# A decode kernel of four layers on one core: GELU as one activation, norms from two sums, first queries by pairs, and w4 with consecutive rows per partition

## The chip, the core and the metric

The kernel runs on one core of one Trainium2 chip. The metric is the time of one execution on the device in microseconds (us); shorter is better. The engines that matter here are PE (TensorE, matmuls; its weight loads stand apart as PEld), DVE (VectorE), ACT (ScalarE), and SP (SyncE), which here only issues transfers (DMAs) from the chip's main memory (HBM) into the on-chip memory (SBUF). Matmuls write PSUM, the accumulator memory.

## The reference

One token of 640 numbers passes through four layers: attention over a cache, a mixer, the same attention again, the same mixer again.

```python
x = x + A(layernorm(x)); x = x + B(layernorm(x))
x = x + A(layernorm(x)); x = x + B(layernorm(x))

# A: W = 4096 last cache rows, 32 heads of 192
q = x @ wq
p = softmax(einsum(q, k_cache[W]) * 192 ** -0.5)
return einsum(p, v_cache[W]) @ wo

# B: with one position the shifted parts of the first half are zero,
# so x1 = x, and what is left is
return x + gelu(layernorm(x) @ w3, approximate=True) @ w4     # w3 640x1536, w4 1536x640
```

Weights, caches and x are bf16. K and V of one head's window are 1.5 MB each.

## The kernel before, in words

**Slots and transfers.** The on-chip memory holds 15 slots of 1.5 MB (`slot`, each 128 partitions by 6144 bf16), one tile `half` of half that size, and two tiles for wo. All large transfers are issued by SP, in one order, which `plan` writes down: for each group of four heads the next group's K between this group's V, wo of the group after its second V, and w3 and w4 (`load_w34`, L131 to L144) last. A load (L111 for K and V) is issued when its slot has come free; SP waits there, and everything behind it on SP waits too. The queue behind SP works through the loads one after the other. Between uses `half` holds the softmax's scratch, the queries Q8 and the output O_sb; at the end of an attention it takes the last rows of w4.

**Attention.** It walks over eight groups of four heads. `qproj` makes a group's queries: 30 matmuls (L288) of 128x128 pieces of wq with one column, a mask (Xq, L292), a spreading matmul (Qrep, L296) and Q8 (L299). DVE turns K over in two halves per head (L311), `kmm` makes the scores (L351, 12 matmuls per head, each on a quarter of PE's columns; even and odd heads use different quarters). `soft_a` to `soft_c` make the softmax of the four heads, `pv_rows` multiplies with V (L458), `evac_rows` scales and turns the result, and `outproj` multiplies with wo (L521), summing over all groups in y_ps. The last group of an attention does its last two heads by `pv_cols` (L432, L443), whose result `evac_cols` scales (L471 to L475). The second attention walks the groups backwards and starts with the last group of the first, whose K (already turned over) and V have stayed in their slots; for these four heads the scores need no transfer, only the queries, and each head that is done frees a slot for a next K.

**Norms.** `ln_tot` takes three sums over the 640 numbers: the mean on DVE (L236), the squares on ACT (L239) and the negative mean on ACT (L241, Identity); a matmul with ones (L243) adds them over the partitions. The variance is completed by tensor_scalar on DVE (L256, L264, L268), and its inverse root by Ln and Exp on ACT (L248, L250). The mixer has two norms in a row, with two such pairs.

**Mixer.** 60 matmuls with w3 (L627) give the 1536 hidden values as 12 columns hT_ps; seven instructions on ACT and DVE make their GELU from Square and Exp (L632 to L640); 60 matmuls with w4 (L644) follow, 36 from a slot and the last 24 from `half`. w3 piece (kc, fc) is 128 consecutive columns; w4 row fc*128 + p lies in partition p, 12 separate rows per partition. The first w3 slot comes free when hT_ps is done, the second after y2T.

ACT's table set is loaded once (L159).

Of the kernel before, what the change touches and what calls it, by code (L numbers as in the profile page):

```python
# [16 lines left out]
P = 128  # L17
G = 4
ACT_TABLE_SET = 6
GELU_C = 0.044715  # L20
GELU_A = -2.0 * (2.0 / 3.141592653589793) ** 0.5
NSLOTS = 15
# [3 lines left out]
def kernel(  # L26
# [14 lines left out]
    nc = tc.nc  # L41
    _, _, D = A_x.shape
# [22 lines left out]
    eps = 1e-5  # L65
# [14 lines left out]


    x_bf = const.tile([ND, P], BF16, name="x_bf")
    nc.scalar.dma_start(x_bf[:], A_x.rearrange("a b (n p) -> (a b n) p", p=P))
# [74 lines left out]

    nc.scalar.add_instruction(mybir.InstLoadActFuncSet(  # L159
        name=nc.get_next_instruction_name(), act_func_set_id=ACT_TABLE_SET, ins=[], outs=[]))  # L160
    ident = const.tile([P, P], F32, name="ident")
# [70 lines left out]

    def ln_tot(src, neg):
        stats = sm.tile([P, 3], F32, tag="ln_stats", name="stats")
# [7 lines left out]
        tot_ps = psm.tile([P, 3], F32, tag="psm", name="tot_ps")  # L242
        nc.tensor.matmul(tot_ps[:], lhsT=ones[:], rhs=stats[:], start=True, stop=True)  # L243
        return tot_ps

    def inv_sqrt(tot_ps, bias, a, name):
        lnv = sm.tile([P, 1], F32, tag=name + "_ln", name="lnv")
        nc.scalar.activation(lnv[:], tot_ps[:, 1:2], ACTF.Ln, bias=bias[:], scale=a)  # L248
# [4 lines left out]
    def ln_stats(src):  # L253
        tot_ps = ln_tot(src, 1.0)
        nt = sm.tile([P, 1], F32, tag="ln_nt", name="nt")
        nc.vector.tensor_scalar(  # L256
            out=nt[:], in0=tot_ps[:, 0:1], scalar1=tot_ps[:, 2:3], scalar2=eps,
            op0=ALU.mult, op1=ALU.add)
        return tot_ps, inv_sqrt(tot_ps, nt, 1.0, "ln_rstd")

    def ln_ln_stats(src):
        tot_ps = ln_tot(src, 1.0 + eps)
        n2 = sm.tile([P, 1], F32, tag="ln_n2", name="n2")
        nc.vector.tensor_scalar(  # L264
            out=n2[:], in0=tot_ps[:, 0:1], scalar1=tot_ps[:, 2:3], scalar2=eps * eps,
            op0=ALU.mult, op1=ALU.add)
        nt = sm.tile([P, 1], F32, tag="ln_nt", name="nt")
        nc.vector.tensor_scalar(  # L268
            out=nt[:], in0=n2[:], scalar1=1.0 / (1.0 + eps), scalar2=eps - eps * eps / (1.0 + eps),
            op0=ALU.mult, op1=ALU.add)  # L270
        r2 = inv_sqrt(tot_ps, n2, 1.0 + eps, "ln_r2")
        return tot_ps, inv_sqrt(tot_ps, nt, 1.0, "ln_rstd"), r2

# [6 lines left out]
    Q_t = {}  # L280
    nq = [0]

    def qproj(g, xn_bf):
# [182 lines left out]

    def evac_cols(g, pr):
        osb, rl = sm.tile([P, 2, 3], BF16, name="osb"), sx[g]["rl"]
        osb_t[g] = osb
        O_ps = Oc_t[g][:, 0:8].rearrange("p (a b) -> p a b", a=2)  # L470
        nc.vector.tensor_tensor(  # L471
            out=osb[:, pr, 0:3:2], in0=O_ps[:, pr, 0:4:3], in1=rl[:, 2 * pr:2 * pr + 2], op=ALU.mult)
        nc.vector.tensor_tensor(
            out=osb[0:TB, pr, 1:2], in0=O_ps[0:TB, pr, 1:2], in1=rl[0:TB, 2 * pr:2 * pr + 1], op=ALU.mult)
        nc.vector.tensor_tensor(  # L475
            out=osb[TB:P, pr, 1:2], in0=O_ps[TB:P, pr, 2:3], in1=rl[TB:P, 2 * pr + 1:2 * pr + 2], op=ALU.mult)

# [38 lines left out]

    def outproj(g, pr, y_ps, first, last):
        osb = osb_t[g]
        for t in range(3):
            for n in range(ND):  # L520
                nc.tensor.matmul(  # L521
                    y_ps[:, n:n + 1], lhsT=wo_t[g][:, 3 * pr + t, n * P:(n + 1) * P],
                    rhs=osb[:, pr, t:t + 1],
                    start=(first and t == 0 and n == 0), stop=(last and t == 2),
                    skip_group_check=True)


    def attention(order, xT_cur, xT_new, keep, loads):
# [23 lines left out]
        tot_ps, rstd = ln_stats(xT_cur)  # L552
        xn_bf = sm.tile([P, ND], BF16, name="xn_bf")
# [19 lines left out]
        for n, g in enumerate(order[:-1]):  # L573
# [19 lines left out]
            if ahead_h is not None:  # L593
                outproj(g, 0, y_ps, n == 0, False)
                outproj(g, 1, y_ps, False, False)
# [4 lines left out]
        outproj(g, 0, y_ps, False, False)  # L600
        outproj(g, 1, y_ps, False, False)
        ahead("wo", gz)
# [13 lines left out]
    def mixer(xT_cur, xT_new):  # L616
# [13 lines left out]
        free.append(mlp["ab"][0])  # L630
        gu = sm.tile([P, NF], F32, name="gu")
        nc.scalar.activation(gu[:], hT_ps[:], ACTF.Square)  # L632
# [7 lines left out]
        nc.vector.tensor_tensor(out=hT[:], in0=ge[:], in1=hT_ps[:], op=ALU.mult)  # L640
        y2T_ps = psm.tile([P, ND], F32, tag="psm", name="y2T_ps")
# [28 lines left out]
    x2 = const.tile([P, ND], F32, name="x2")  # L670
    mixer(x1, x2)
    for g in first[:-2]:
# [6 lines left out]
    x4 = const.tile([P, ND], F32, name="x4")  # L679
    mixer(x3, x4)  # L680

# [35 lines left out]
```

## Time and profile before

| what | value |
|---|---|
| median of 3 runs | 534.06 us (533.92 to 534.87) |
| profiled execution | 534.18 us, span in the profile 532.3 us |
| busy share of the span | PE 59%, PEld 28%, DVE 53%, ACT 7% |
| DMA | 218.76 MB, mean 411 GB/s |
| mean granted TensorE clock | 0.672 |
| K and V loads | 60 each, 1.5 MB, 28.1 us from issue to landing (median) |

The span is cut into 40 slices of 13.3 us; a row of digits gives the busy tenths in each. The chain of waits follows the work that ended last back from the end, at each step to what released it. In a group or a timeline, a line reads: start, duration, engine, line of the program, operation, what it writes and reads, shapes, count, and in brackets how long the engine had been idle and who released it. "Issue to landing" is the time from SP's issue of a transfer to the moment its last byte is there. Durations of matmuls are modelled and overlap; the starts tell the rate.

### The profile page before, as it was taken

The page shows a single profiled execution, that of the slowest core. Times are in us where ns is not written, and L with a number is a line of the kernel's source. Part 1 is how long each engine was busy: PE and PEld are TensorE (multiplying, and loading weights), DVE is VectorE, ACT ScalarE, POOL GpSimd, SP SyncE. Part 2 cuts the span into 40 slices and gives each one's busy share as a digit, 9 for nine tenths or more (in the row PEclk, how much of TensorE's full clock was granted, in tenths as well). Part 3 has the DMA queues.
Part 4 walks back from the last instruction along what each step waited for, and adds up shares of the span by engine and source line. Part 5 has one row for each costly group of instructions (what it writes and reads, how often), then busy time and mean ns, then how long its engine had stood idle before and what let it go on. Part 6 is the DMA issues. An engine that isn't in the chain of part 4 may idle for free.

```text
span 532.3 us, 8132 instructions
## 1 busy us (share of the span) xinstructions
PE 316.7 (59%) x3597; PEld 151.1 (28%) x3597; DVE 280.6 (53%) x413; ACT 36.3 (7%) x113; POOL 2.1 (0%) x11
## 2 busy tenths in 40 slices
PE   1154756584656747555576677766565657454674
PEld 0011223141322313222155323333321314122254
DVE  4176565465645557264422476775736447365322
ACT  1001010010100001010011101010101001010011
POOL 1000000000000000000000000000000000000000
PEclk9998766656576665757665776768665765657655
DMA  8999999999999999999999899999999999999995
GB/s 348 428 426 423 420 428 424 428 423 425 422 425 426 422 424 426 424 425 422 422 407 338 326 415 428 421 424 425 423 425 422 426 428 423 423 425 425 420 406 193
DMA packets 26151, 218.76 MB, mean 411 GB/s; under 512 B 2692, under 2 KB 7300, under 8 KB 10116
## 3 DMA queue, kind: packets, MB, share of 16 engines
q1 hardware_dynamic: 26106, 218.25, 98.4%
q8 instruction: 28, 0.46, 0.3%
q14 instruction: 7, 0.06, 0.0%
q10 hardware_dynamic: 10, 0.00, 0.0%
HBM read 218.24 MB, written 0.00 MB: 410 GB/s over the span
## 4 chain that ended last, share of the span: by engine, by line
DMA 71%; PE 14%; DVE 12%; issue 1%; ACT 1%; SPq 0%; DVEq 0%
DMA slot<-in_A_v_cache_dram 37%; DMA slot<-in_A_k_cache_dram 34%; DVE slot L311 8%; PE S_ps L351 7%; PE y_ps L521 1%; PE qT_ps L288 1%; PE O_ps L458 1%; PE O_ps L432 1%; PE O_ps L443 1%; PE hT_ps L627 1%; PE y2T_ps L644 1%; DVE pm L367 1%; DVE half L389 0%; SPq L104 0%; PE OX_ps L496 0%
## 5 line engine op out<-in xcount | busy, mean ns | idle before, releaser
L311 DVE STREAM_TRANSPOSE slot<-slot 128x1536 uint32<-128x1536 uint32 x120 | 206.8, 1755 | 80.1 <-DMA slot<-in_A_k_cache_dram 80.1
L351 PE MATMUL S_ps<-slot,half 128*8 128x512 bf16 x768 | 172.6, 565 | 113.7 <-DVE slot L311 112.0
L351 PEld LDWEIGHTS <-half 128*8 128x8 bf16 x768 | 46.6, 104 | 204.1 <-issue 194.2
L458 PE MATMUL O_ps<-slot,half 128*8 128x384 bf16 x512 | 58.9, 432 | 0.0
L458 PE MATMUL O_ps<-slot,PT 128*8 128x384 bf16 x448 | 51.0, 463 | 0.0
L367 DVE TENSOR_REDUCE pm<-S_ps 128x1 f32<-128x512 f32 x16 | 11.1, 691 | 42.5 <-PE S_ps L351 42.5
L381 ACT COPY nb_sb<-nb_ps 128x1 f32<-128x1 f32 x16 | 2.5, 159 | 424.6 <-PE nb_ps L379 424.6
L292 DVE TENSOR_TENSOR Xq<-qT_ps,maskq 128x24 bf16<-128x24 f32 x16 | 2.9, 179 | 54.0 <-PE qT_ps L288 54.0
L458 PEld LDWEIGHTS <-half 128*8 128x8 bf16 x512 | 19.4, 97 | 18.3 <-issue 15.0
L288 PE MATMUL qT_ps<-xn_bf,slot 128*128 128x1 bf16 x480 | 15.2, 164 | 13.5 <-DMA slot<-in_A_wq_dram 11.2
L496 PE MATMUL OX_ps<-half,hoX 128*128 128x192 f32 x26 | 13.1, 608 | 15.4 <-DVE half L490 15.4
L521 PE MATMUL y_ps<-osb,wo_g 128*128 128x1 bf16 x480 | 15.5, 165 | 10.5 <-DVE osb L502 9.2
L458 PEld LDWEIGHTS <-PT 128*8 128x8 bf16 x448 | 15.7, 102 | 18.1 <-issue 16.1
L521 PEld LDWEIGHTS <-wo_g 128*128 128x128 bf16 x480 | 16.0, 105 | 16.0 <-issue 15.3
L288 PEld LDWEIGHTS <-slot 128*128 128x128 bf16 x480 | 13.7, 98 | 21.6 <-DMA slot<-in_A_wq_dram 12.8
L371 PE MATMUL pmT_ps<-ident,pmh 128*4 128x128 f32 x16 | 5.3, 334 | 18.1 <-DVE pmh L369 18.1
L389 DVE STREAM_TRANSPOSE half<-half 128x512 bf16<-128x512 bf16 x16 | 11.2, 701 | 4.6 <-ACT half L383 4.6
L398 PE MATMUL Pp_ps<-half,identb 128*32 128x32 bf16 x256 | 6.7, 235 | 11.6 <-DVE half L389 11.6
L498 DVE TENSOR_TENSOR half<-OX_ps,m 128x192 f32<-128x192 f32 x13 | 4.6, 357 | 14.3 <-PE OX_ps L496 14.3
L379 PE MATMUL nb_ps<-ngm,hsT 4*128 4x1 f32 x32 | 8.1, 319 | 6.0 <-DVE ngm L373 6.0
L398 PEld LDWEIGHTS <-identb 128*32 128x32 bf16 x256 | 6.1, 116 | 18.9 <-issue 18.8
L496 PEld LDWEIGHTS OX_ps<-half,hoX 128*128 128x128 f32 x26 | 6.5, 311 | 16.5 <-DVE half L490 16.5
(122 smaller groups left out, 170.2 us busy)
## 6 DMA issues: line engine op xcount, KB each, us to landing
slot<-in_A_k_cache_dram SPq DMA_DIRECT2D x60, 1536.0 KB, 28.1
slot<-in_A_v_cache_dram SPq DMA_DIRECT2D x60, 1536.0 KB, 28.1
wo_g<-in_A_wo_dram SPq DMA_DIRECT2D x14, 960.0 KB, 28.1
slot<-in_A_wq_dram SPq DMA_DIRECT2D x5, 1536.0 KB, 13.0
slot<-in_B_w_dram SPq DMA_DIRECT2D x2, 1536.0 KB, 23.5
slot<-in_B_w_dram SPq DMA_DIRECT2D x2, 1120.0 KB, 19.5
half<-in_B_w_dram SPq DMA_DIRECT2D x2, 640.0 KB, 8.6
slot<-in_B_w_dram SPq DMA_DIRECT2D x2, 384.0 KB, 17.5
```

The lines of the kernel that those rows point to most:

```text
L288: nc.tensor.matmul(qT_ps[:, tl:tl + 1], lhsT=wq_t[kc][:, t * P:(t + 1) * P], rhs=xn_bf[:, kc:kc + 1], start=(kc == 0), stop=(kc == ND - 1))
L311: nc.vector.transpose(T[:, hf * HALF:(hf + 1) * HALF].bitcast(U32).rearrange("p (f j k) -> p j f k", f=NFB, j=HJ, k=32), Kn[:, hf * HALF:( ...
L351: nc.tensor.matmul(S_ps[r:r + 8, :], lhsT=Q_t[g][:, x, par * NCOL + 2 * f + t, :], rhs=Tv[:, f, :, t], start=(x == 0 and n == 0), stop=(n ...
L367: nc.vector.tensor_reduce(out=pm[:], in_=S_t[g][:], op=ALU.max, axis=AX.X)
L379: nc.tensor.matmul(nb_ps[:], lhsT=hsT[0:G, :], rhs=sx[g]["ngm"][0:G, :], start=True, stop=True)
L389: nc.vector.transpose(ET.rearrange("p (j r) -> p j r", r=32), E.rearrange("p (j k) -> p j k", k=32))
L398: nc.tensor.matmul(two, lhsT=identb[:, 32 * tl:32 * (tl + 1)], rhs=ETv[:, :, 0:2, m].rearrange("p (j e) x -> p x j e", e=2), start=True, s ...
L432: nc.tensor.matmul(O_ps[:, pr, ca:ca + 1], lhsT=V[:, j * Dh + oa:j * Dh + oa + P], rhs=col(j), start=(j == 0), stop=(j == J - 1))
L443: nc.tensor.matmul(O_ps[:, pr, cc:cc + 1], lhsT=V[:, j * Dh + oc - r0:j * Dh + oc - r0 + P], rhs=col(j), start=False, stop=(j == js[-1]), ...
L458: nc.tensor.matmul(O_t[g][r:r + 8, :], lhsT=PT[:, i, jj, :], rhs=V[:, jj * 2 * Dh:(jj + 1) * 2 * Dh], start=(i == 0 and jj < 4), stop=(i = ...
L496: nc.tensor.matmul(OX_ps[:], lhsT=hoX[:].rearrange("p h i -> p (h i)"), rhs=O_sb, start=True, stop=True)
L521: nc.tensor.matmul(y_ps[:, n:n + 1], lhsT=wo_t[g][:, 3 * pr + t, n * P:(n + 1) * P], rhs=osb[:, pr, t:t + 1], start=(first and t == 0 and ...
```

## The change

- **GELU**: the seven instructions become one activation (Gelu_apprx_tanh). It needs another table set, so ACT's table is loaded after the second norm, and loaded back after the GELU (not in the last mixer).
- **Norms**: two sums for three; the product of the mean with itself is taken from the same column, with a constant tile (eps1, eps2) added. In the mixer xnn is made before the second inverse root. A factor that was folded into the Identity's scale is now the activation's scale (ln2_scale).
- **First queries by pairs**: only at the start of the second attention, the queries of heads 0 and 1 are made, head 0's scores, then the queries of heads 2 and 3, head 1's scores, the second pair's spread, and the scores of heads 2 and 3.
- **Last columns**: of the last group's second pair, `evac_cols` scales one head at a time, and the first third of its 15 wo matmuls moves ahead of the last head's columns.
- **w4** is loaded as 12 consecutive rows per partition, in two transfers (9216 and 6144 bytes per partition) where there were four, in pieces of 256 to 1280 bytes. So hidden value 12 p + fc must lie in partition p, and w3's pieces are taken with a step of 12 columns.

```diff
-        nc.sync.dma_start(
-            b[:, F:FB4].rearrange("p (k n) -> p k n", n=D),
-            B_w4[0:NB4 * P, :].rearrange("(k p) n -> p k n", p=P))
-        nc.sync.dma_start(b[:, FB4:FREE], B_w4[NB4 * P:(NB4 + 1) * P, 0:FREE - FB4])
-        nc.sync.dma_start(half[:, 0:D - P], B_w4[NB4 * P:(NB4 + 1) * P, P:D])
-        nc.sync.dma_start(
-            half[:, D - P:HALF].rearrange("p (k n) -> p k n", n=D),
-            B_w4[(NB4 + 1) * P:NF * P, :].rearrange("(k p) n -> p k n", p=P))
+        w4 = B_w4.rearrange("(p k) n -> p (k n)", p=P)
+        nc.sync.dma_start(b[:, F:FREE], w4[:, 0:FREE - F])
+        nc.sync.dma_start(half[:], w4[:, FREE - F:NF * D])
...
-        return a[:, kc * F + fc * P:kc * F + (fc + 1) * P] if kc < NKA else b[:, fc * P:(fc + 1) * P]
+        return a[:, kc * F + fc:(kc + 1) * F:NF] if kc < NKA else b[:, fc:F:NF]
...
-        junk2 = sm.tile([P, ND], F32, tag="ln_junk2", name="junk2")
-        nc.scalar.activation(junk2[:], src[:], ACTF.Identity, scale=-neg / D, accum_out=stats[:, 2:3])
...
+    def inv_sqrt(tot_ps, add, name):
+        nt = sm.tile([P, 1], F32, tag=name + "_nt", name="nt")
+        nc.vector.scalar_tensor_tensor(
+            out=nt[:], in0=tot_ps[:, 0:1], scalar=tot_ps[:, 0:1], in1=add[:], op0=ALU.mult, op1=ALU.subtract,
+            reverse1=True)
...
+    def qpair_a(g, x, xn_bf):
+        qT_ps = psm.tile([P, NOC // 2], F32, tag="psm", name="qT_ps")
+        for tl in range(NOC // 2):
+            t = g * NOC + x * (NOC // 2) + tl
+            for kc in range(ND):
+                nc.tensor.matmul(
+                    qT_ps[:, tl:tl + 1], lhsT=wq_t[kc][:, t * P:(t + 1) * P], rhs=xn_bf[:, kc:kc + 1],
+                    start=(kc == 0), stop=(kc == ND - 1))
+        Xq = sm.tile([P, NOC // 2, 4], BF16, name="Xq")
...
+        return Xq
+
+    def qpair_b(g, x, Xq):
+        Qrep_ps = psm.tile([P, 2 * NCOL], F32, tag="psm", name="Qrep_ps")
+        nc.tensor.matmul(Qrep_ps[:], lhsT=Lb[:].rearrange("p a i -> p (a i)"), rhs=Xq[:].rearrange("p t b -> p (t b)"), start=True, stop=True)
...
+        nc.vector.tensor_tensor(
+            out=Q_t[g][:, x], in0=Qrep_ps[:, :].unsqueeze(2).broadcast_to([P, 2 * NCOL, 8]),
+            in1=blk8[:, x, :].unsqueeze(1).broadcast_to([P, 2 * NCOL, 8]), op=ALU.mult)
...
-        qproj(g0, xn_bf)
-        for i in range(G):
-            keys(g0 * G + i)
-            kmm(g0, i)
-            if not warm and i == 0:
-                qproj(g1, xn_bf)
         if warm:
+            qpair_b(g0, 0, qpair_a(g0, 0, xn_bf))
+            kmm(g0, 0)
+            Xq = qpair_a(g0, 1, xn_bf)
+            kmm(g0, 1)
+            qpair_b(g0, 1, Xq)
+            kmm(g0, 2)
+            kmm(g0, 3)
             need(G + 1)
...
         evac_rows(gz)
-        outproj(gz, 0, y_ps, False, False)
+        outproj(gz, 0, y_ps)
+        evac_cols(gz, 0)
+        outproj(gz, 1, y_ps, chunks=(0,))
         ahead("V", gz * G + 3)
         pv_cols(gz, 3, kept(gz, 3))
         evac_cols(gz, 1)
-        outproj(gz, 1, y_ps, False, True)
+        outproj(gz, 1, y_ps, last=True, chunks=(2, 1))
...
-        tot1, rstd1, rstd2 = ln_ln_stats(xT_cur)
+        tot1 = ln_tot(xT_cur)
+        rstd2 = inv_sqrt(tot1, eps2, "ln_r2")
         xnn = sm.tile([P, ND], BF16, name="xnn")
         ln_apply(xnn, xT_cur, tot1, rstd2)
+        rstd1 = inv_sqrt(tot1, eps1, "ln_rstd")
+        table(GELU_SET)
...
-        gu = sm.tile([P, NF], F32, name="gu")
-        nc.scalar.activation(gu[:], hT_ps[:], ACTF.Square)
-        nc.vector.tensor_scalar(out=gu[:], in0=gu[:], scalar1=GELU_C, scalar2=1.0, op0=ALU.mult, op1=ALU.add)
-        nc.vector.tensor_tensor(out=gu[:], in0=gu[:], in1=hT_ps[:], op=ALU.mult)
-        ge = sm.tile([P, NF], F32, name="ge")
-        nc.scalar.activation(ge[:], gu[:], ACTF.Exp, scale=GELU_A)
-        nc.vector.tensor_scalar_add(ge[:], ge[:], 1.0)
-        nc.vector.reciprocal(ge[:], ge[:])
         hT = sm.tile([P, NF], BF16, name="hT")
-        nc.vector.tensor_tensor(out=hT[:], in0=ge[:], in1=hT_ps[:], op=ALU.mult)
+        nc.scalar.activation(hT[:], hT_ps[:], ACTF.Gelu_apprx_tanh, scale=ln2_scale)
+        if not last:
+            table(LN_EXP_SET)
```

More of the change, by code (lines that the diff above doesn't have):

```diff
@@ L18 @@
 G = 4
-ACT_TABLE_SET = 6
-GELU_C = 0.044715
-GELU_A = -2.0 * (2.0 / 3.141592653589793) ** 0.5
+LN_EXP_SET = 6
+GELU_SET = 11
 NSLOTS = 15
@@ L79 @@
     ctx.enter_context(tc.manual_schedule())
+    eps1 = const.tile([P, 1], F32, name="eps1")
+    nc.vector.memset(eps1[:], eps)
+    eps2 = const.tile([P, 1], F32, name="eps2")
+    nc.vector.memset(eps2[:], eps * eps / (1.0 + eps))
+    ln2_scale = (1.0 + eps) ** -0.5
     x_bf = const.tile([ND, P], BF16, name="x_bf")
@@ L156, in w4_at, with table @@
         return t[:, o + n * P:o + (n + 1) * P]
-    nc.scalar.add_instruction(mybir.InstLoadActFuncSet(
-        name=nc.get_next_instruction_name(), act_func_set_id=ACT_TABLE_SET, ins=[], outs=[]))
+    def table(n):
+        nc.scalar.add_instruction(mybir.InstLoadActFuncSet(
+            name=nc.get_next_instruction_name(), act_func_set_id=n, ins=[], outs=[]))
+    table(LN_EXP_SET)
     ident = const.tile([P, P], F32, name="ident")
@@ L231, with ln_tot @@
     nc.vector.tensor_copy(xT[:], xT_ps[:])
-    def ln_tot(src, neg):
-        stats = sm.tile([P, 3], F32, tag="ln_stats", name="stats")
+    def ln_tot(src):
+        stats = sm.tile([P, 2], F32, tag="ln_stats", name="stats")
         junk0 = sm.tile([P, ND], F32, tag="ln_junk0", name="junk0")
@@ L239, in ln_tot @@
         nc.scalar.activation(junk[:], src[:], ACTF.Square, scale=float(D) ** -0.5, accum_out=stats[:, 1:2])
-        junk2 = sm.tile([P, ND], F32, tag="ln_junk2", name="junk2")
-        nc.scalar.activation(junk2[:], src[:], ACTF.Identity, scale=-neg / D, accum_out=stats[:, 2:3])
-        tot_ps = psm.tile([P, 3], F32, tag="psm", name="tot_ps")
+        tot_ps = psm.tile([P, 2], F32, tag="psm", name="tot_ps")
         nc.tensor.matmul(tot_ps[:], lhsT=ones[:], rhs=stats[:], start=True, stop=True)
         return tot_ps
-    def inv_sqrt(tot_ps, bias, a, name):
+    def inv_sqrt(tot_ps, add, name):
[3 more added lines that the diff above has]
+            reverse1=True)
         lnv = sm.tile([P, 1], F32, tag=name + "_ln", name="lnv")
-        nc.scalar.activation(lnv[:], tot_ps[:, 1:2], ACTF.Ln, bias=bias[:], scale=a)
+        nc.scalar.activation(lnv[:], tot_ps[:, 1:2], ACTF.Ln, bias=nt[:])
         rstd = sm.tile([P, 1], F32, tag=name, name="rstd")
@@ L251, in inv_sqrt @@
         return rstd
[L253 to L272, printed above, removed]
     def ln_apply(dst, src, tot_ps, rstd):
@@ L281 @@
     nq = [0]
+    def qpair_a(g, x, xn_bf):
[8 more added lines that the diff above has]
+        nc.vector.tensor_tensor(
+            out=Xq[:], in0=qT_ps[:, :].unsqueeze(2).broadcast_to([P, NOC // 2, 4]),
+            in1=maskq[:, :].unsqueeze(1).broadcast_to([P, NOC // 2, 4]), op=ALU.mult)
+        return Xq
+    def qpair_b(g, x, Xq):
+        Qrep_ps = psm.tile([P, 2 * NCOL], F32, tag="psm", name="Qrep_ps")
+        nc.tensor.matmul(Qrep_ps[:], lhsT=Lb[:].rearrange("p a i -> p (a i)"), rhs=Xq[:].rearrange("p t b -> p (t b)"), start=True, stop=True)
+        if x == 0:
+            Q_t[g] = Q8_two[nq[0] % 2]
+            nq[0] += 1
+        nc.vector.tensor_tensor(
+            out=Q_t[g][:, x], in0=Qrep_ps[:, :].unsqueeze(2).broadcast_to([P, 2 * NCOL, 8]),
+            in1=blk8[:, x, :].unsqueeze(1).broadcast_to([P, 2 * NCOL, 8]), op=ALU.mult)
     def qproj(g, xn_bf):
@@ L465, with evac_cols @@
     osb_t = {}
-    def evac_cols(g, pr):
-        osb, rl = sm.tile([P, 2, 3], BF16, name="osb"), sx[g]["rl"]
-        osb_t[g] = osb
+    def evac_cols(g, odd):
+        if not odd:
+            osb_t[g] = sm.tile([P, 2, 3], BF16, name="osb")
+        osb, rl = osb_t[g], sx[g]["rl"]
         O_ps = Oc_t[g][:, 0:8].rearrange("p (a b) -> p a b", a=2)
+        t, c, r0 = (2, 3, TB) if odd else (0, 0, 0)
         nc.vector.tensor_tensor(
-            out=osb[:, pr, 0:3:2], in0=O_ps[:, pr, 0:4:3], in1=rl[:, 2 * pr:2 * pr + 2], op=ALU.mult)
+            out=osb[:, 1, t:t + 1], in0=O_ps[:, 1, c:c + 1], in1=rl[:, 2 + odd:3 + odd], op=ALU.mult)
         nc.vector.tensor_tensor(
-            out=osb[0:TB, pr, 1:2], in0=O_ps[0:TB, pr, 1:2], in1=rl[0:TB, 2 * pr:2 * pr + 1], op=ALU.mult)
-        nc.vector.tensor_tensor(
-            out=osb[TB:P, pr, 1:2], in0=O_ps[TB:P, pr, 2:3], in1=rl[TB:P, 2 * pr + 1:2 * pr + 2], op=ALU.mult)
+            out=osb[r0:r0 + TB, 1, 1:2], in0=O_ps[r0:r0 + TB, 1, 1 + odd:2 + odd],
+            in1=rl[r0:r0 + TB, 2 + odd:3 + odd], op=ALU.mult)
     def norm_rows(g):
@@ L515, in evac_rows, with outproj @@
         nc.vector.tensor_copy(osb[:], OT_ps[:])
-    def outproj(g, pr, y_ps, first, last):
+    def outproj(g, pr, y_ps, first=False, last=False, chunks=(0, 1, 2)):
         osb = osb_t[g]
-        for t in range(3):
+        for t in chunks:
             for n in range(ND):
@@ L523, in outproj @@
                     rhs=osb[:, pr, t:t + 1],
-                    start=(first and t == 0 and n == 0), stop=(last and t == 2),
+                    start=(first and t == chunks[0] and n == 0), stop=(last and t == chunks[-1]),
                     skip_group_check=True)
@@ L550, in keys @@
                 trans_end(h)
-        tot_ps, rstd = ln_stats(xT_cur)
+        tot_ps = ln_tot(xT_cur)
+        rstd = inv_sqrt(tot_ps, eps1, "ln_rstd")
         xn_bf = sm.tile([P, ND], BF16, name="xn_bf")
@@ L557, in attention @@
         warm = g0 * G in T_t
-        qproj(g0, xn_bf)
-        for i in range(G):
-            keys(g0 * G + i)
-            kmm(g0, i)
-            if not warm and i == 0:
-                qproj(g1, xn_bf)
-        if warm:
-            need(G + 1)
+        if warm:
+            qpair_b(g0, 0, qpair_a(g0, 0, xn_bf))
[5 more added lines that the diff above has]
+            kmm(g0, 3)
+            need(G + 1)
+        else:
+            qproj(g0, xn_bf)
+            for i in range(G):
+                keys(g0 * G + i)
+                kmm(g0, i)
+                if i == 0:
+                    qproj(g1, xn_bf)
         soft_a(g0)
@@ L593, in attention @@
             if ahead_h is not None:
-                outproj(g, 0, y_ps, n == 0, False)
-                outproj(g, 1, y_ps, False, False)
+                outproj(g, 0, y_ps, first=(n == 0))
+                outproj(g, 1, y_ps)
         gz = order[-1]
@@ L599, in attention @@
             pv_rows(gz, i, kept(gz, i), n_heads=2)
-        outproj(g, 0, y_ps, False, False)
-        outproj(g, 1, y_ps, False, False)
+        outproj(g, 0, y_ps)
+        outproj(g, 1, y_ps)
         ahead("wo", gz)
@@ L614, in attention, with mixer @@
         nc.vector.tensor_tensor(out=xT_new[:], in0=xT_cur[:], in1=y_ps[:], op=ALU.add)
-    def mixer(xT_cur, xT_new):
-        tot1, rstd1, rstd2 = ln_ln_stats(xT_cur)
+    def mixer(xT_cur, xT_new, last):
+        tot1 = ln_tot(xT_cur)
+        rstd2 = inv_sqrt(tot1, eps2, "ln_r2")
         xnn = sm.tile([P, ND], BF16, name="xnn")
         ln_apply(xnn, xT_cur, tot1, rstd2)
+        rstd1 = inv_sqrt(tot1, eps1, "ln_rstd")
+        table(GELU_SET)
         xn = sm.tile([P, ND], F32, name="xn")
@@ L630, in mixer @@
         free.append(mlp["ab"][0])
-        gu = sm.tile([P, NF], F32, name="gu")
-        nc.scalar.activation(gu[:], hT_ps[:], ACTF.Square)
-        nc.vector.tensor_scalar(out=gu[:], in0=gu[:], scalar1=GELU_C, scalar2=1.0, op0=ALU.mult, op1=ALU.add)
-        nc.vector.tensor_tensor(out=gu[:], in0=gu[:], in1=hT_ps[:], op=ALU.mult)
-        ge = sm.tile([P, NF], F32, name="ge")
-        nc.scalar.activation(ge[:], gu[:], ACTF.Exp, scale=GELU_A)
-        nc.vector.tensor_scalar_add(ge[:], ge[:], 1.0)
-        nc.vector.reciprocal(ge[:], ge[:])
         hT = sm.tile([P, NF], BF16, name="hT")
-        nc.vector.tensor_tensor(out=hT[:], in0=ge[:], in1=hT_ps[:], op=ALU.mult)
+        nc.scalar.activation(hT[:], hT_ps[:], ACTF.Gelu_apprx_tanh, scale=ln2_scale)
+        if not last:
+            table(LN_EXP_SET)
         y2T_ps = psm.tile([P, ND], F32, tag="psm", name="y2T_ps")
@@ L670 @@
     x2 = const.tile([P, ND], F32, name="x2")
-    mixer(x1, x2)
+    mixer(x1, x2, False)
     for g in first[:-2]:
@@ L679 @@
     x4 = const.tile([P, ND], F32, name="x4")
-    mixer(x3, x4)
+    mixer(x3, x4, True)
     row_ps = psm.tile([ND, P], F32, tag="psm", name="row_ps")
```

## The prediction

> **What bounds the kernel now.** I read the page from part 2 down: the slices, then the chain of waits, then short stretches and the timeline where the slices dip. Word for word, first from the page:
>
> ```profile
> DMA  8999999999999999999999899999999999999995
> GB/s 348 428 426 423 420 428 424 428 423 425 422 425 426 422 424 426 424 425 422 422 407 338 326 415 428 421 424 425 423 425 422 426 428 423 423 425 425 420 406 193
> ...
> DMA 71%; PE 14%; DVE 12%; issue 1%; ACT 1%; SPq 0%; DVEq 0%
> ```
>
> The transfers bind: 420 to 428 GB/s in nearly every slice, and 71% of the chain is DMA. They are not full in three places: the first slice, slices 20 to 22 (first mixer and restart of attention) and the last slice (second mixer). The change touches the last two. Against 423 GB/s the restart loses some 6.5 us, so an edit there pays only if it closes this hole or shortens the tail.
>
> The stretches (us; per engine busy us and count; then clock, DMA share, GB/s) place the hole:
>
> ```profile
> 290.00:292.00 2.00, 1.51 (x57) 1.42 (x54) 0.33 (x3) 0.26 (x3) 0.00 (x0) 0.50 0.99 418
> ...
> 296.00:298.00 2.00, 2.00 (x16) 0.62 (x20) 0.00 (x0) 0.00 (x0) 0.00 (x0) 0.50 0.57 240
> 298.00:300.00 2.00, 2.00 (x32) 0.84 (x26) 0.00 (x0) 0.00 (x0) 0.00 (x0) 0.74 0.54 92
> 300.00:302.00 2.00, 0.85 (x13) 0.17 (x3) 0.92 (x2) 0.00 (x0) 0.00 (x0) 1.00 0.66 283
> 302.00:304.00 2.00, 1.36 (x33) 1.11 (x32) 1.82 (x2) 0.94 (x3) 0.00 (x0) 1.00 0.98 418
> ```
>
> The queue is empty from 296 to 302: the third load after the mixer waits for a slot that the scores S_ps (L351) of a kept head free. From 302 on it is full to the end, so what moves there moves the end.
>
> The timeline of the second mixer, between its two matmul groups:
>
> ```profile
> 523.99 1.74 PE L627 MATMUL hT_ps<-xnn,slot 128*128 128x1 bf16 x60 [1.42 <-DVE xnn L275]
> ...
> 525.76 0.18 ACT L632 ACTIVATE gu<-hT_ps 128x12 f32<-128x12 f32 x1 [2.02 <-PE hT_ps L627]
> ...
> 527.48 1.10 PE L644 MATMUL y2T_ps<-hT,slot 128*128 128x1 bf16 x36 [1.75 <-DVE hT L640]
> ...
> 528.44 0.78 PE L644 MATMUL y2T_ps<-hT,half 128*128 128x1 bf16 x24
> ```
>
> Seven small steps fill 525.76 to 527.48. But w4's last rows (tile half) are issued at 519.4 and land 8.8 later, at 528.2: 0.25 ahead of their first use. In the first mixer 282.2 plus 8.4 is 290.5, used at 290.73. **A faster chain meets w4 almost at once.**
>
> **The mixer's chain.** (a) The Identity sum goes: 0.20 in the chain. (b) xnn started after the second Ln (L248) though its own Exp was done 0.16 earlier; now it is emitted ahead: 0.16. The new sum (a scalar_tensor_tensor on one column) has no row; L264 on one column took 0.23 and L490, the same operation on 192, 0.42; I take 0.23, at most 0.2 worse. (c) GELU: 1.72 from 525.76 to 527.48 becomes one activation of 128x12 from PSUM, 0.19 like L632, and the 0.14 of handover that the chain shows ahead of L644: 0.33, so 1.39 gone. (d) The table load: L159 took 1.28. Its way is xnn's start 285.46 (first mixer, 0.36 earlier), the second sum behind xnn 286.0, Ln and Exp to 286.5, table to 287.8; hT_ps ends at 287.7. So 0.1 shows. The load back runs beside y2T (1.75). Compute alone: 0.20 + 0.16 + 1.39 - 0.1 = 1.65 earlier in each mixer.
>
> **w4's landing.** w3's last row lands at 285.4 and 522.9 (issue plus 17.0 and 18.0), w4's last at 290.5 and 528.2: 5.1 to 5.3 us for 1.97 MB in pieces of 256 to 1280 bytes. K and V, in pieces of 12 KB, land 1.57 MB each 3.7 us; at that rate w4, now in pieces of 9 and 6 KB, takes 4.6. So it lands 0.5 earlier (bounds: 0, and 0.9 if it also stops trailing on a slow engine). SP's issues fall from six to four; L140's took 11.5 us on a full queue, but what it holds back stands behind the same bytes, so nothing more. half's matmuls then start just behind the landing, 0.5 + 0.2 = **0.7 earlier in each mixer**, not 1.65; 0.95 of the compute gain is lost, and is cover for (d).
>
> **w3's weights at a step of 12.** No row reads weights at a step. Below: no change, 27 ns from one L627 load to the next, as for every 128-column bf16 group (L288, L521, L644); faster is excluded, since count and columns stay. Above: the fp32 128-column weights of L243 start 0.19 apart, 9.8 us more per mixer. The nearest for a stepped read are L398's moving operands, 32 columns 64 bytes apart: 16 matmuls in 0.41, four side by side, 0.1 per round against 27 ns for 32 packed columns at L351's rate (512 in 0.43). That round includes weight loads and dispatch, so it allows a read at the same rate or some two to four times slower. L627 is the same kind of instruction as now, so I take 27 ns as likeliest, weakly. The Trainium skill speaks against it: "SBUF — State Buffer", Specifications (TRN2), asks for two hits in each 16-byte line for full rate, and 24 bytes make one; by that the time would be the first rival's. Its "TensorE: Matmul & The Clock Gate", Weight-path perf modes, lets the fast weight load take steps up to 1,024; by that my sum stands.
>
> **Norm and queries of the second attention.** Identity: 0.20. Half of 30 query matmuls: 15 x 27 ns = 0.41. Q8 with 96 columns for 192 (0.36; Xq's 24 took 0.18): 0.11. So scores start 0.7 + 0.2 + 0.5 = 1.45 earlier, at 294.5, and the third load, now issued at 298.70, goes 1.45 earlier too. But the four heads' 48 matmuls took 4.80 because heads of a pair run side by side. Now 15 full-width query matmuls stand between heads 0 and 1, and the spread (Qrep) between 1 and 2. A single head takes 2.72, its last 0.2 overlapped: 2.5. Then 0.4 of queries; head 1 in 2.5 at clock 0.50 or 1.3 at 1.00, middle 1.9; Qrep and Q8 0.55; heads 2 and 3 side by side 2.0. Sum 7.35 (6.6 to 8.0), 2.55 more. **The scores of this group end 1.1 later** (-1.45 + 2.55). Who waits: softmax, K's transposes, and the sixth load after the mixer (310.06, the first V), whose slot a head of the next group frees:
>
> ```profile
> L111 SPq DMA_DIRECT2D slot<-in_A_k_cache_dram x1: 328/328/328, 298.7 to 298.7; - x1
> ...
> DMA to landing us min/median/max: 6.2/6.2/6.2
> ```
>
> ```profile
> L111 SPq DMA_DIRECT2D slot<-in_A_v_cache_dram x1: 328/328/328, 310.1 to 310.1; - x1
> ...
> DMA to landing us min/median/max: 7.4/7.4/7.4
> ```
>
> On an empty queue a load lands after 6.2, the sixth after 7.4: it has 1.2 to spare and slips 1.1. So what the earlier third load gains (1.45) is given back at the sixth: the stream comes 0.1 earlier (0.85 earlier to 0.5 later over the range). The next load has 9.8, so nothing else starves.
>
> **At nothing:** the first norm and two memsets, beside 22.4 us of waiting for K at the start; five output matmuls (0.14) moved ahead of the last head's columns, where PE is busy back to back from 518.24 to 520.3, so they cost there what they save behind (uncovered: 0.14).
>
> **Sum.** Stream -0.1, tail -0.7 (what the first mixer gains is inside the stream's -0.1): **-0.85 us**. Own time of the profiled execution is 534.18 (span 532.3 and 1.9 around it); the median is 534.06, so 533.3 there and **533.2** on the median.
>
> **Rivals.**
> - Half-rate weights: 60 x 27 ns = 1.6 more. Mixer -0.36 + 1.6 - 1.39 = -0.15, w4 no longer binds; scores end -0.15 - 0.2 - 0.5 + 2.55 = +1.7, less 1.2 spare: +0.5; tail -0.15. Total +0.3: 534.4. For it: the 24-byte step; against: nothing in the trace. Chance 0.25.
> - **Slower: the step loses the fast weight path.** At four times, 107 ns, 4.8 more per mixer: mixer +3.05, stream +3.05 - 0.7 + 2.55 - 1.2 = +3.7, tail +3.05: 540.8. Each ns per load is 0.12 us in all, so it is slower than now from 51 ns and by over 0.2% from some 60 ns. Chance 0.15.
> - The clock stays at 0.50 through the pairs: 9.5 for the scores, stream +2.0, total +1.3: 535.3. Against it: the clock rose to 1.00 at 299, after 3 us of scores. Chance 0.07.
> - A table switch that costs more than its row. Up to 0.95 is covered by the wait for w4, beyond that both mixers pay. The trace has one load, followed by 5.3 us in which ACT has nothing to do, so it shows no follow-up cost. At twice the row, 1.28 more, 0.33 is lost twice: 533.9. Chance 0.06. The Trainium skill ("ScalarE: Activation LUTs", What ACT_TABLE_LOAD costs) adds a drain of 1.38 to each switch; by that the time would be 534.1.
>
> **How the numbers follow.** Forecast 0.47; a measurement of this kernel can tell 0.2% (1.07 us) from no change. Forecast alone spans 532.4 (scores in 6.6, w4 0.9 earlier) to 533.9; some half of it is beyond 0.2%. Faster: 0.25 from it and 0.02 from the mildest ends of the clock's and the table's cases, 0.27. Same: 0.22, the half rate's 0.2 and the table's 0.05, 0.47. Slower: 0.15, the clock's 0.06, the half rate's rest 0.05: 0.26. The range runs from 532.3 to 536.3 (weights at 70 ns: 0.3 + 16 x 0.12 = 2.2), leaving out mainly the lost weight path.
>
> **What would show it.** L627's group: 1.74 if the step is free, 3.3 at half rate, 6 or more without the fast path. ACT idle between table load and Gelu. y2T's half part starting right at w4's landing. Scores L351 at the restart: 7.35 for 4.80, with the sixth load landing 6.2 after issue. I am wrong above all if L627 grows, or if the sixth load is on time after all.

## The result and the profile after

The changed kernel takes 536.09 us (median of 9 runs), the kernel before 534.42 in the same sessions: a ratio of 1.0028, 95% interval 1.0019 to 1.0037, or **1.5 us slower** (1.0 to 2.0). The profiled execution took 536.5 us with a span of 534.7, 2.4 more than the one before. The forecast was 0.9 us faster.

The page of the changed kernel, its DMA share and GB/s by slice:

```profile
DMA  8999999999999999999997979999999999999994
GB/s 347 429 426 423 424 426 425 427 425 425 425 426 427 421 426 423 427 423 424 421 406 299 391 309 427 425 424 425 427 424 425 425 427 424 424 427 424 420 407 187
```

Where there was one dip there are two. Slice 21 falls from 338 to 299 (the first w3 slot comes free 1.2 us later), slice 22 rises from 326 to 391 (bytes held up in slice 21 move there, and the third load after the mixer is issued at 297.7 for 298.7), and slice 23, nearly full before, falls from 415 to 309.

The second mixer in the timeline of the changed kernel (columns as in the prediction):

```profile
525.94 3.60 PE L650 MATMUL hT_ps<-xnn,slot 128*128 128x1 bf16 x60 [1.27 <-DVE nt L249]
...
529.58 0.18 ACT L655 ACTIVATE hT<-hT_ps 128x12 bf16<-128x12 f32 x1 [1.83 <-PE hT_ps L650]
529.81 1.10 PE L661 MATMUL y2T_ps<-hT,slot 128*128 128x1 bf16 x36 [0.27 <-ACT hT L655]
...
530.77 0.78 PE L661 MATMUL y2T_ps<-hT,half 128*128 128x1 bf16 x24
```

The GELU is short: 0.23 us from its start to y2T, where there were 1.72. But hT_ps takes 3.60 us for 1.74, with the same 60 matmuls: the step of 12 columns doubles the time of a weight load, from 27 to 58 ns.

The scores of the first group of the second attention, on PE, first in the kernel before, then in the changed one:

```profile
295.94 4.78 PE L351 MATMUL S_ps<-slot,half 128*8 128x512 bf16 x48 [0.45 <-DVE half L299]
```

```profile
294.97 2.73 PE L359 MATMUL S_ps<-slot,half 128*8 128x512 bf16 x12 [0.35 <-DVE half L287]
297.63 0.56 PE L272 MATMUL qT_ps<-xn_bf,slot 128*128 128x1 bf16 x15
298.12 2.66 PE L359 MATMUL S_ps<-slot,half 128*8 128x512 bf16 x12
300.71 0.18 PE L283 MATMUL Qrep_ps<-Xq,Lb 128*128 128x12 bf16 x1
301.24 1.98 PE L359 MATMUL S_ps<-slot,half 128*8 128x512 bf16 x24 [0.35 <-DVE half L287]
```

They begin 1.0 earlier than before and end 2.5 later (303.2 for 300.7): heads 0 and 1, side by side before, stand behind one another with the queries between them, and take 5.8 us.

What the transfers do then, in stretches of 2 us, first of the kernel before, then of the changed one (the last two columns are DMA share and GB/s):

```profile
310.00:312.00 2.00, 1.94 (x15) 0.58 (x8) 1.32 (x1) 0.00 (x0) 0.00 (x0) 0.50 1.02 375
312.00:314.00 2.00, 2.00 (x32) 0.93 (x29) 0.00 (x0) 0.00 (x0) 0.00 (x0) 0.83 0.98 412
```

```profile
308.00:310.00 2.00, 1.65 (x21) 0.92 (x22) 1.97 (x4) 0.59 (x1) 0.00 (x0) 0.50 1.08 451
310.00:312.00 2.00, 2.00 (x18) 0.63 (x16) 1.93 (x4) 0.00 (x0) 0.00 (x0) 0.50 0.21 86
312.00:314.00 2.00, 1.94 (x18) 0.70 (x14) 1.81 (x2) 0.00 (x0) 0.00 (x0) 0.50 0.43 74
314.00:316.00 2.00, 2.00 (x32) 0.89 (x29) 0.00 (x0) 0.00 (x0) 0.00 (x0) 0.94 0.82 332
```

The queue runs nearly empty for some 4 us: the sixth load after the mixer, issued at 310.06 before, comes at 312.55. The load itself in the changed kernel:

```profile
L116 SPq DMA_DIRECT2D slot<-in_A_v_cache_dram x1: 328/328/328, 312.6 to 312.6; - x1
...
DMA to landing us min/median/max: 6.1/6.1/6.1
```

It lands in the time of an empty queue. The eighth load landed at 324.9 before (issued at 313.5) and lands at 327.6 now (315.6), the last V at 518.1 (495.7) and at 520.7 (499.2): the hole of 310 to 315 is carried to the end.

### The profile page after: what moved, and what is told of

The parts are those of the page before. It is cut to its first block, busy times and chain, and to the rows that moved or that the text cites. A ratio compares the mean times of both kernels' runs of the same rounds, so it can differ in the third digit from the quotient of the medians.

```text
span 534.7 us, 8117 instructions
## 1 busy us (share of the span) xinstructions
PE 318.0 (59%) x3598; PEld 152.3 (28%) x3598; DVE 279.4 (52%) x409; ACT 39.2 (7%) x106; POOL 2.1 (0%) x11
## 4 chain that ended last, share of the span: by engine, by line
DMA 71%; PE 15%; DVE 11%; issue 1%; ACT 1%; SPq 0%; DVEq 0%
DMA slot<-in_A_v_cache_dram 37%; DMA slot<-in_A_k_cache_dram 34%; DVE slot L319 8%; PE S_ps L359 7%; PE O_ps L466 2%; PE hT_ps L650 1%; PE O_ps L440 1%; PE O_ps L451 1%; PE y2T_ps L661 1%; PE qT_ps L296 1%; PE y_ps L530 1%; DVE pm L375 1%; SPq L109 0%; DVE half L397 0%; PE tot_ps L244 0%
## 5 line engine op out<-in xcount | busy, mean ns | idle before, releaser
L359 PE MATMUL S_ps<-slot,half 128*8 128x512 bf16 x768 | 170.7, 548 | 115.9 <-DVE slot L319 114.0
L359 PEld LDWEIGHTS <-half 128*8 128x8 bf16 x768 | 44.5, 102 | 206.9 <-issue 194.0
L466 PEld LDWEIGHTS <-half 128*8 128x8 bf16 x512 | 19.4, 96 | 18.3 <-issue 14.5
## 6 DMA issues: line engine op xcount, KB each, us to landing
slot<-in_A_wq_dram SPq DMA_DIRECT2D x5, 1536.0 KB, 11.2
half<-in_B_w_dram SPq DMA_DIRECT2D x2, 768.0 KB, 10.1
```

The lines of the kernel that those rows point to most:

```text
L359: nc.tensor.matmul(S_ps[r:r + 8, :], lhsT=Q_t[g][:, x, par * NCOL + 2 * f + t, :], rhs=Tv[:, f, :, t], start=(x == 0 and n == 0), stop=(n ...
L466: nc.tensor.matmul(O_t[g][r:r + 8, :], lhsT=PT[:, i, jj, :], rhs=V[:, jj * 2 * Dh:(jj + 1) * 2 * Dh], start=(i == 0 and jj < 4), stop=(i = ...
```

## The experiments

**Theory.** Two parts cost: the weights' step, 1.9 us per mixer, and the pairs, through the end of the group's scores, which the whole stream of transfers follows one for one. By the stream I mean the transfers up to the last V, by the tail what comes between the last V's landing and the last y2T matmul. **Rivals.** The slow hT_ps alone makes the stream late, by freeing w3's slot later, and the pairs are harmless (they have the spare that I predicted); or the table switches cost more than their row. I call the GELU, norms and last columns G, the pairs Q, and w3's step with w4's rows W. In the table, the difference is the ratio's times 534.4 us; the scores, the clock's rise (how long after the scores' begin the granted clock goes from 0.50 to 1.00) and the last V's landing are of one profile each.

| kernel | parts | ratio (95%) | us against before | scores us, end | clock's rise | last V landed |
|---|---|---|---|---|---|---|
| before | | | | 4.8, 300.7 | 3.1 | 518.1 |
| neither | G | 0.9974 (0.9962 to 0.9985) | -1.4 | 5.2, 300.1 | 4.1 | 517.3 |
| pairs_only | Q | 1.0045 (1.0031 to 1.0059) | +2.4 | 8.3, 303.9 | 5.6 | 521.5 |
| w_only | W | 1.0077 (1.0065 to 1.0090) | +4.1 | 5.5, 303.2 | 4.7 | 521.0 |
| old_w | G, Q | 1.0007 (0.9998 to 1.0016) | +0.4 | 7.1, 301.5 | 2.6 | 519.1 |
| no_pairs | G, W | 1.0002 (0.9992 to 1.0012) | +0.1 | 5.4, 300.8 | 4.5 | 518.2 |
| changed | G, Q, W | 1.0028 (1.0019 to 1.0037) | +1.5 | 8.3, 303.2 | 5.6 | 520.7 |

**no_pairs.** The edit, in the changed kernel:

```diff
+        qproj(g0, xn_bf)
+        for i in range(G):
+            keys(g0 * G + i)
+            kmm(g0, i)
...
         if warm:
-            qpair_b(g0, 0, qpair_a(g0, 0, xn_bf))
-            kmm(g0, 0)
-            Xq = qpair_a(g0, 1, xn_bf)
-            kmm(g0, 1)
-            qpair_b(g0, 1, Xq)
-            kmm(g0, 2)
-            kmm(g0, 3)
...
```

> The changed kernel with the first queries of the second attention made at once again (30 matmuls, then the scores of four heads); all else as changed. My theory: the pairing alone makes the four heads' scores take 8.3 us for 4.8, they end 2.5 us late, and the transfers, which have no spare there, end 2.5 us late with them. Without it the second attention starts 0.25 (mixer) + 0.2 (norm) earlier, the stream by as much, the tail by 0.25: 0.7 us faster than the kernel before, S_ps in 4.8 us. Rival: the stream is late because w3's slot is freed 1.2 us later by the slow hT_ps and the queue stands empty from 286 to 291; then undoing the pairs changes little and the time stays 1 to 2 us above the kernel before.

Measured: 534.46 us, no difference to before (1.0002), 1.4 us better than the changed kernel. The rival falls: hT_ps is as slow as in the changed kernel, and w3's slot comes as late, but the last V lands 2.4 us earlier. My number was 0.8 too good; in this profile the scores took 5.4, not 4.8, and so ended at the time of before: the TensorE clock rose to 1.00 only 4.5 us after they began (3.1 in the kernel before).

**old_w.** load_w34 and w3_at as in the kernel before, all else as changed.

> The changed kernel with w3's packed columns and w4's rows loaded as before; GELU, norms and pairs as changed. My theory: hT_ps back to 1.75 us, but w4's last rows, landing as late as before, hold the mixer's gain at 0.2 us; the pairs still cost 3.4 us of scores less 0.5 of start, so the stream is some 2.5 us late: 2.2 us slower than the kernel before, hardly better than the changed kernel. Rival (the slow hT_ps makes the stream late): with it gone the time falls below the kernel before by about 1 us.

Measured: 534.69 us, 0.4 above before, where I expected 2.2. The direction holds (it does not fall below before, as the rival has it), the size does not: the scores took 7.1 us, not 8.3. In this profile the clock rose 2.6 us after the scores began, in the changed kernel after 5.6. So a second profile was taken of both.

> The kernel old_w once more, for a second profile. In its first the TensorE clock rose to 1.00 some 2.7 us after the group's scores began, and they took 7.1 us; in the changed kernel it rose after 5.6 us, and they took 8.3. If the time of that rise is free from run to run: another rise here, scores between 6.6 and 8.3 us that are longer the later it rises, and a run time that follows. If it belongs to the kernel: 7.1 us again and a rise after 2.7.

> The changed kernel once more, for a second profile. If the time of the clock's rise is free from run to run: scores of 6.6 to 8.3 us by the rise. If it belongs to the kernel: 8.3 us again with the rise 5.6 us after their begin.

old_w: the clock rose after 4.0, the scores took 7.5 us, the run 535.05 us (0.4 more than its median). The changed kernel: 5.7, 8.3 and 536.53 again. The rise is not fixed for old_w, and the time went the way of the scores; whether it is free in the changed kernel too, two profiles don't tell. In every trace here the clock changes only on a grid of 3.41 us; counted from the program's start, that grid lay 1.5 us apart in old_w's two profiles, but 0.1 apart in the changed kernel's.

All profiles together part the two effects. Without pairs (seven profiles) the scores take longer the later the clock rises, from 4.8 us at a rise after 3.1 to 5.7 at 5.2; with pairs (five) from 7.1 at 2.6 to 8.3 at 5.7. At a rise after about 4.1 they take 5.2 and 7.5. So at the same rise the pairs cost 2.3 us; the rest of the 3.5 by which the scores grew from before to changed, some 1.2, goes with the later rise. Whether the pairs have a part in that later rise, the profiles don't tell.

**neither.** Both edits together.

> The changed kernel with both the pairs and the w3/w4 layout undone: only the GELU, the norms and the last columns. My theory: the compute of each mixer is 1.7 us shorter but waits for w4's last rows, which gives 0.2 us per mixer, and 0.2 for the norm: 0.6 us faster than the kernel before, with y2T's half part starting right after w4 lands. If w4's landing does not hold it: some 3.5 us faster. If table switches cost more than their 1.28 us: no sign of it here up to 1.4 us, since the wait for w4 covers it.

Measured: 533.06 us, **1.4 us faster** than before (0.6 expected). Its second mixer:

```profile
523.37 1.28 ACT L165 ACT_TABLE_LOAD   x1
...
524.66 0.18 ACT L652 ACTIVATE hT<-hT_ps 128x12 bf16<-128x12 f32 x1
...
525.28 1.12 PE L658 MATMUL y2T_ps<-hT,slot 128*128 128x1 bf16 x36 [0.70 <-DMA slot<-in_B_w_dram]
...
526.26 0.24 PE L658 MATMUL y2T_ps<-hT,half 128*128 128x1 bf16 x4
...
527.32 0.69 PE L658 MATMUL y2T_ps<-hT,half 128*128 128x1 bf16 x20 [0.81 <-DMA half<-in_B_w_dram]
```

PE waits twice for w4, 0.70 and 0.81 us (in the first mixer 0.86 and 0.86): this is where most of the GELU's gain goes. The tail from the last V to the last y2T matmul is 0.5 us shorter, where I had 0.2: half's first 4 pieces come with an earlier transfer, so 20 matmuls, not 24, follow the last landing. The rest of the surplus is not explained in full: in this profile the first mixer began 0.7 earlier than in the one of before, ahead of anything the mixer's edits touch. Of that 0.4 is there when the first loads land (the first wq load, issued at 0.74 in both, at 6.96 for 7.32; the first K at 25.37 for 25.75), which the edits do not explain; whether it is chance stays open. And the table load ends at 524.65 and Gelu starts at 524.66: the switch cost its 1.28 us and nothing more, and in step2_no_pairs below, where the load also ends just before Gelu, y2T starts 0.23 us after Gelu's start, as in the changed kernel, where the load had ended 1.8 us earlier. That rival falls. The Trainium skill, "ScalarE: Activation LUTs", What ACT_TABLE_LOAD costs, adds a drain of some 1.38 us to each switch; no such time stands between load and Gelu here, and the measurement decides.

**pairs_only.** The pairs in the kernel before (qpair_a and qpair_b added, and the first edit of this section backwards).

> The kernel before with the queries by pairs alone. My theory: scores start 0.5 us earlier, take 8.2 us for 4.8, and end 2.9 us later; the sixth load after the mixer is issued 2.9 later, the queue has no spare there, and the whole time grows by 2.9 us. If the sixth load has the 1.2 us of spare that I predicted from its 7.4 us to landing: 1.7 us. If the earlier third load decides: 0.5 us faster.

Measured: 537.58 us, 2.4 slower (1.7 to 3.2); scores 8.3 us, ending 3.2 later (some 1.2 of it with the clock's later rise). Its stretches:

```profile
310.00:312.00 2.00, 1.66 (x11) 0.49 (x11) 1.90 (x6) 0.00 (x0) 0.00 (x0) 0.50 0.51 215
312.00:314.00 2.00, 2.00 (x22) 0.85 (x17) 2.00 (x2) 0.00 (x0) 0.00 (x0) 0.50 0.01 6
314.00:316.00 2.00, 1.94 (x14) 0.45 (x10) 0.53 (x1) 0.00 (x0) 0.00 (x0) 0.76 0.73 252
```

With nothing else changed, the hole behind the fifth load opens: 6 GB/s at 312 to 314, 412 before. The sixth load slips 3.2 (313.3 for 310.1), the last V 3.4. The time's interval alone would allow 1.7; the profile does not allow the spare.

**w_only.** load_w34 and w3_at of the changed kernel in the kernel before.

> The kernel before with w3 at a step of 12 columns and w4's consecutive rows alone. My theory: hT_ps takes 3.65 us for 1.75 in each mixer, nothing covers it, w4 lands 0.5 us earlier but is not waited for: the stream 1.9 us later, the tail 1.9 us longer, 3.8 us slower than the kernel before. If the earlier w4 or the shorter transfers help the stream: under 3 us.

Measured: 538.94 us, 4.1 slower (3.5 to 4.8), hT_ps 3.67 us. Here nothing covers the slow weights, and each mixer pays them whole, 1.8: the scores begin that much later (297.7) and the tail is that much longer. The scores end 2.5 later, 0.7 of it with the clock's later rise, and the last V lands 2.9 later. Beside G they cost only 1.5 (no_pairs against neither), because there PE would wait for w4 anyway and w4 lands earlier: from the last V to w4's last row 9.4 us in the changed kernel, 10.1 before.

**steps.** The weights' step by itself:

```diff
-        for fc in range(NF):
+        s1, s2, s3 = mlp["steps"]
+        w_at = lambda kc, fc, s: mlp["ab"][0][:, kc * P + fc:kc * P + fc + (P - 1) * s + 1:s]
+        for fc in range(4):
             for kc in range(ND):
...
+                nc.tensor.matmul(hT_ps[:, fc:fc + 1], lhsT=w_at(kc, fc, s1), rhs=xnn[:, kc:kc + 1], start=(kc == 0), stop=(kc == ND - 1))
...
+    mlp["steps"] = (2, 4, 6)
     mixer(x1, x2)
...
+    mlp["steps"] = (8, 7, 24)
     mixer(x3, x4)
```

> A measurement of the weights' step alone, on the kernel before: hT_ps's 60 matmuls take their weights from the first w3 slot at a step of 2, 4 and 6 columns (first mixer) and of 8, 7 and 24 columns (second), 20 matmuls each on a line of their own; so the hidden values are of other columns, and the output is not the reference's. If two elements in a 16-byte line are enough: 0.53 us per 20 matmuls at steps 2 and 4, 1.2 us at 8 and 24, steps 6 and 7 between or like 8. If any step above one column halves the rate: 1.2 us for all six. If the cost grows with the step: 24 clearly above 8.

The first mixer, steps 2, 4, 6, then the second, steps 8, 7, 24:

```profile
286.14 0.68 PE L629 MATMUL hT_ps<-xnn,slot 128*128 128x1 bf16 x20 [1.42 <-DVE xnn L275]
286.67 0.82 PE L632 MATMUL hT_ps<-xnn,slot 128*128 128x1 bf16 x20
287.36 1.07 PE L635 MATMUL hT_ps<-xnn,slot 128*128 128x1 bf16 x20
```

```profile
525.20 1.35 PE L629 MATMUL hT_ps<-xnn,slot 128*128 128x1 bf16 x20 [1.42 <-DVE xnn L275]
526.41 1.22 PE L632 MATMUL hT_ps<-xnn,slot 128*128 128x1 bf16 x20
527.49 1.54 PE L635 MATMUL hT_ps<-xnn,slot 128*128 128x1 bf16 x20
```

Columns 0 to 3 take the first step of a mixer, 4 to 7 the second, 8 to 11 the third. From start to start, divided by 20: 27 ns at step 2, 34 at 4; 60 at 8, 54 at 7. The last group of each has no follower: its duration less one matmul's 0.165, over 19, gives 48 ns at step 6 and 72 at 24. With 58 at 12: free at 2, rising almost evenly from 4 to 8, and little beyond (12 is no slower than 8). None of the three expectations is quite right. The Trainium skill, "SBUF — State Buffer", Specifications (TRN2), wants two hits in each 16-byte line; step 2 keeps four and is free, step 8 keeps one and is not, as it says; but step 4 keeps two and already costs a quarter more.

**step4_no_pairs.** Changed kernel without pairs, w4 in three blocks of 4 consecutive rows per partition, w3 at a step of 4.

```diff
-        return a[:, kc * F + fc:(kc + 1) * F:NF] if kc < NKA else b[:, fc:F:NF]
+        R = 4
+        o = fc // R * P * R + fc % R
+        t, o = (a, kc * F + o) if kc < NKA else (b, o)
+        return t[:, o:o + (P - 1) * R + 1:R]
```

> The changed kernel without the pairs, and w4 with 4 consecutive rows per partition in three blocks (pieces of 5120, 4096, 1024 and 5120 bytes), so that w3's weights are taken with a step of 4 columns, 8 bytes, not 24. If a step halves the rate only when each element lies in another 16-byte line (two elements per line are enough): hT_ps takes 1.75 us, w4's last rows land some 0.9 us earlier than in the kernel before, and the time is 2.0 us below the kernel before (stream 1.1, tail 0.9). If any step above one column halves it: hT_ps 3.65 us and the time of the kernel without pairs, 0.7 us below.

Measured: 532.96 us, 0.9971 (0.9960 to 0.9982), 1.6 faster; hT_ps 2.1 us, between the two expectations. Not to be told from neither.

**pairs_side.** old_w with the pairs in another order.

```diff
             kmm(g0, 0)
-            Xq = qpair_a(g0, 1, xn_bf)
             kmm(g0, 1)
-            qpair_b(g0, 1, Xq)
+            qpair_b(g0, 1, qpair_a(g0, 1, xn_bf))
             kmm(g0, 2)
```

> The changed kernel with w3/w4 as before (the kernel old_w) and another order of the pairs: queries and spread of heads 0 and 1, both heads' scores, then queries and spread of heads 2 and 3, and their scores. So heads 0 and 1 can run side by side again, and only the second pair's queries stand between. My theory (the end of the transfers follows the end of this group's scores one for one): scores start 0.5 us earlier than without pairs and take some 6.3 us for 4.8, so they end 1.0 us later: 1.0 us slower than the kernel with neither, 0.4 us faster than the kernel before, with the stream 1.0 us behind the one of neither. If what costs is not the order on TensorE but the pairs' extra spread and steps: like old_w, 1.8 us slower than neither. If the first freed slot decides: as fast as neither or 0.5 us faster.

```profile
294.29 3.52 PE L364 MATMUL S_ps<-slot,half 128*8 128x512 bf16 x24 [0.35 <-DVE half L292]
...
299.05 1.99 PE L364 MATMUL S_ps<-slot,half 128*8 128x512 bf16 x24 [0.35 <-DVE half L292]
```

Heads 0 and 1 together again take 3.5 us, not 5.8. Scores end 0.9 later than in neither, the last V lands 1.0 later, and the time is 534.05 us, 1.0001 (0.9991 to 1.0011): 1.4 above neither by the ratios (1.0 expected). The intervals do not part it from old_w; the profile does: its scores took 6.8 us for old_w's 7.1, though the clock rose later (after 3.3 us for 2.6). That rise came 0.2 before the first two heads were done, so their 3.5 is a time at 0.50, like the 2.73 and 2.66 that one head takes by itself in the changed kernel.

**step2_no_pairs.** w4's rows two and two, w3 at a step of 2, and half's last two row pairs as two transfers.

> The changed kernel without pairs, with w4's rows two and two (pieces of 2560 bytes, and 1536 and 1024 where a row pair is cut), so that w3's weights are taken at a step of 2 columns, which took 27 ns as packed ones do, and with the last two pieces of half as two transfers. My theory: hT_ps 1.75 us, w4 lands 0.3 us earlier than with rows one by one, and 10 matmuls instead of 20 follow the last landing (0.27 us): 0.3 to 0.6 us below the kernel with neither, some 1.8 us below the kernel before. If w4's last landing does not bind: no difference to neither (1.4 us below).

Measured: **532.22 us, 0.9958 (0.9944 to 0.9972), 2.2 us faster than before**, the fastest of all. Its last matmuls:

```profile
525.67 0.77 PE L664 MATMUL y2T_ps<-hT,half 128*128 128x1 bf16 x14
526.80 0.42 PE L664 MATMUL y2T_ps<-hT,half 128*128 128x1 bf16 x10 [0.36 <-DMA half<-in_B_w_dram]
```

PE still waits for w4 at the end, but 0.36 for 0.81, and 10 matmuls follow the landing, not 20. Against neither it is 0.9 us; the intervals overlap a little.

## Why the prediction was wrong, step by step

- **"w3's weights at a step of 12": failed.** I took 27 ns as likeliest; it is 58. This is the half-rate rival, to which I gave 0.25, and the Trainium skill's "SBUF — State Buffer", Specifications (TRN2), which spoke for it, was right on the direction.
- **"It has 1.2 to spare": failed.** The sixth load had nothing to spare. I compared two issue-to-landing times, 7.4 and 6.2. The sixth load itself did land only 1.2 later (318.7 for 317.5), as 2.5 less 1.2 has it; but what stood behind it came 2.7 later. And "full to the end" from 302 on was read from stretches that stop at 304. In stretches of 0.5 us, first of the kernel before, then of the changed one:

```profile
311.50:312.00 0.50, 0.50 (x4) 0.14 (x2) 0.00 (x0) 0.00 (x0) 0.00 (x0) 0.50 0.81 246
312.00:312.50 0.50, 0.50 (x4) 0.14 (x2) 0.00 (x0) 0.00 (x0) 0.00 (x0) 0.50 0.75 319
```

```profile
310.50:311.00 0.50, 0.50 (x4) 0.13 (x2) 0.50 (x1) 0.00 (x0) 0.00 (x0) 0.50 0.12 49
311.00:311.50 0.50, 0.50 (x10) 0.16 (x8) 0.50 (x1) 0.00 (x0) 0.00 (x0) 0.50 0.06 25
```

Already before, the stream thins out to 246 and 319 GB/s (418 in the stretch ahead) where the sixth load's bytes take over: it came just in time. In the changed kernel a DMA share of 0.06 at 25 GB/s, what one engine of 16 alone comes to, goes on when the others have run dry. Such a laggard makes a landing late: the fourth load had landed 5.2 after the third (310.1 and 304.9), not 3.7. That it is why the sixth's 7.4 looked like a spare is inferred; that there was no spare is shown, since the last V follows the end of the scores: 2.5 and 2.6 in the changed kernel, 3.2 and 3.4 in pairs_only, 2.5 and 2.9 in w_only.
- **"Sum 7.35 (6.6 to 8.0)": the mechanism was right, the size low.** 8.3: the clock stayed at 0.50 through heads 0 and 1 (2.73 and 2.66), where I had taken head 1 at a middle of 1.9. That the pairs cost 2.3 at the same rise of the clock, close to the 2.55 worked out, speaks for the mechanism. The rival of a clock that stays low (9.5) did not come true either: heads 2 and 3 ran at 1.00.
- **w4's landing, "0.5 earlier": right.** From w3's last row to w4's last 4.6 us (284.9 to 289.5), as worked out; 5.1 before.
- **The chain (a), (b), (c), (d): right.** From the sum of x to hT_ps 2.41 us for 2.75 (0.34 gone, 0.36 worked out); GELU 1.49 gone (1.39); table load covered.
- **"A faster chain meets w4 almost at once": right**, as neither shows by its two waits per mixer (0.70 to 0.86 each).
- **The scores' begin, "1.45 earlier": too early.** It is 1.0, since the slow weights leave 0.26 of the mixer's 0.7 (and 0.7, 0.2 and 0.5 add up to 1.4).
- **At nothing:** nothing in the traces speaks against it; the moved wo matmuls were not tried by themselves.

By the measured terms the sum comes out: stream +2.6, tail 10.9 us for 11.2, -0.3; together +2.3, and the span grew by 2.4. The median grew by less (1.5); the profiled executions are one each. What stays open is how the parts add: Q costs 2.4 alone, 1.8 beside G and 1.4 beside G and W. The clock's rise moved the scores by up to 1.2 between profiles, as much as would explain it, but it was not made to vary by itself.

## What to carry to other kernels

A step in the weights' columns is not free just because the count of columns is the same: here a step of 2 bf16 columns cost nothing and 4 a quarter more, so measure it. Splitting a batch of matmuls to start its first part sooner can cost the side-by-side running of the rest; ask which finish the next consumer waits for, here the last head's, not the first's. A load's time from issue to landing did not tell here how full the queue was: look in short stretches whether the bytes per us fall.

## What the runs showed of the hardware that I had not expected

- A 128-column bf16 weight load, start to start, at a granted clock of 0.50: 27 ns packed and at step 2, 34 at 4, 48 at 6, 54 at 7, 60 at 8, 58 at 12, 72 at 24.
- A switch of ACT's table took the 1.28 us of its row and no more: Gelu started 0.01 us after it (neither, step2_no_pairs).
- After the scores began, the granted clock rose from 0.50 to 1.00 after 2.6 to 5.7 us, and differently in two profiles of the same kernel (2.6 and 4.0); a group's scores change by about 1 us with it. All changes of a trace lie on a grid of 3.41 us.
- When the queue ran dry, about one of the 16 DMA engines was still busy alone (a DMA share of 0.06 at 25 GB/s from 311 to 312 in the changed kernel).
- Two heads' matmuls on different quarters of PE's columns ran side by side: 24 in 3.5 us at a clock of 0.50, where 12 by themselves took 2.7.
